# A layernorm's column factor and shift moved off the input: state weights, skip term and an outer product instead of two VectorE passes

## The chip, the cores and the metric

One core of one Trainium2 chip runs the whole program. The metric is the device time of one execution in microseconds, the median of three runs. All traces are of one profiled execution on that core.

## The reference

The program is one block of a network: a state-space convolution and an MLP mixer, each behind a layernorm that is modulated by a condition vector `c`. Only the first half matters here, with x of 2048 rows by 512 columns:

```python
sa, ca, ga = rows 0, 1, 2 of (silu(c) @ w_mod).reshape(6, 512)
h = layernorm(x) * (1 + ca) + sa
K[d, l] = Re sum_n C[d,n] * exp(dt[d] * A[d,n] * l) * dt[d] * B[d,n]     # 128 states n, 2048 taps l
y = irfft(rfft(pad(h)) * rfft(pad(K))) + h * Dskip                        # along the 2048 rows
x = x + ga * y
# second half: layernorm, a token mixer with w1 and w2, an MLP with w3 and w4
```

`1 + ca`, `sa` and `ga` hold one number for each of the 512 columns d. A factor on column d can stand at h, at K and Dskip, or at y: the convolution is linear in each.

## The kernel before, in words

The program runs in three stages, and each engine executes its instructions in the order in which the code is written (`manual_schedule`). Every engine waits only for what an instruction needs, and for the tile buffer that it writes to come free.

**Prologue (to about 40 us).** It loads and prepares the state parameters: decay rates in `TES`, phases in `T0S` and `T1S`, the magnitudes of the products C·dt·B as `wn`, and the first condition rows (`mods[0]` is sa, `mods[1]` is 1 + ca, `mods[2]` is ga, each spread over 128 partitions).

**The loop over 32 steps k (L554 to L587, about 40 to 213 us).** It makes the kernel K (16 columns of d a step) and, at its side, the first transform of u (16 blocks of 128 rows). In a step:

- `turns(k+2, 0)` and `turns(k+2, 1)`: TensorE forms phases in two PSUM tiles named xx (pool `psx`, two buffers; 8 matmuls for the sine half, 10 for the cosine half), and ScalarE takes their sine into a tile tr (three buffers).
- `products(k)`: VectorE multiplies tr with the magnitudes p into e0 and e1 (two buffers each): two passes on L476, one each on L485 and L486, and on even k one more on L482.
- `burst(k)`: TensorE contracts e0 with e1 in 32 small matmuls (64 in the trace) into a PSUM tile kp; after odd k ScalarE copies kp to KX.
- Every fourth step (k = 1, 5, ... 25, called `fresh`) also makes the next magnitudes: `exps` puts five groups of matmuls through the same two xx buffers, and ScalarE loads its exponential table, makes five tiles p, loads the sine table again, and goes on. The first two groups stand ahead of `burst(k)`, three behind it. `fill` matmuls (L492) stand between them and compute nothing that is used.
- `side[k]` holds work for step k: `u_stats` (mean and variance of a block of u on VectorE, the inverse root on GpSimd), `u_norm` (two VectorE passes, L425 and L426), `u_dft` (matmuls of two normalised blocks with the matrix FU into two PSUM tiles named pu, L435), and three times `mod_parts` and `mod_sum`, which make later condition rows through the same pool. That pool, `psu`, has two buffers; one `u_dft` takes both. The copies out of pu (`evict`, `later`) are ScalarE work written at the start of the next step, followed by SyncE DMAs to the DRAM tile VU.

**Stages two and three** (spectra and inverse transform to about 350 us, then mixer and MLP) are not touched by the change.

In step 1 the kernel before multiplies `mods[1]` and `mods[0]` by `mods[2]` (L584, L585), so that u already carries ga.

Of the kernel before, what the change touches and what calls it, by code (L numbers as in the profile page):

```python
# [27 lines left out]
def shape_constants():  # L28
# [10 lines left out]
    FU = FU.reshape(128, 2, 2, 2, 32).transpose(0, 1, 2, 4, 3)  # L39
    FK = np.zeros((2, 2, 32, 2, 64))  # L40
# [40 lines left out]
    for e in range(16):  # L81
# [8 lines left out]
        FU=FU.reshape(128, 256), FK=FK.reshape(128, 128), T2=T2, T3=T3, G=Gm,  # L90
# [21 lines left out]
def body(ctx, tc, A):  # L112
# [88 lines left out]
    WN = ph.tile([128, 512], F32, name="WN")  # L201
    modu = ph.tile([128, 3, 512], F32, name="modu")
# [82 lines left out]
    with tc.manual_schedule():  # L285
# [15 lines left out]
        Y.dma_start(FK, A["FK"])  # L301
        V.memset(cst, MAGIC)
# [105 lines left out]
        V.tensor_tensor(as4(wn), as4(wn), by(dt), op=OP.mult)  # L408
    pr.close()
# [9 lines left out]
    def u_stats(b):  # L419
        ul[b] = ln_stats(wk, [ut[b // 4][:, b % 4]], "lu")  # L420

    def u_norm(b):
        x = ut[b // 4][:, b % 4]
        mv, r = ul.pop(b)
        V.scalar_tensor_tensor(x, x, mv[:, 0, 0:1], mods[1], op0=OP.subtract, op1=OP.mult)  # L425
        V.scalar_tensor_tensor(x, x, r[:, 0:1], mods[0], op0=OP.mult, op1=OP.add)  # L426

    def u_dft(b, cp2):
        x = ut[b // 4]
        ps = [psu.tile([128, 512], F32, name="pu") for h in range(2)]  # L430
        for i in range(2):
            for h in range(2):
                q = 64 * (1 - i if h == 0 else i)
                j = slice(32 * JB[2 * h + cp2], 32 * JB[2 * h + cp2] + 32)
                T.matmul(ps[h][q:q + 64], FU[j, h, cp2 * 64:cp2 * 64 + 64], x[j, b % 4 + i],  # L435
                         start=True, stop=True, skip_group_check=True)

        def evict():
            vs = uv.tile([128, 2, 512], F32, name="vs")
            for h in range(2):  # L440
                act(vs[:, h], ps[h])
                c0 = h * 32 + cp2 * 16 + (14 - b if h == 0 else b)
                for i in range(2):
                    Y.dma_start(dram(VU, (c0 + i) * 256, [[16384, 64], [1048576, 2], [1, 256]]),
                                vs[i * 64:i * 64 + 64, h].rearrange("p (a d) -> p a d", a=2))
        later.append(evict)
# [22 lines left out]
    def products(k):  # L469
# [7 lines left out]
        if k == 0:  # L477
            weigh(0)
# [47 lines left out]
    at = lambda i: 1 + (i * 28) // 16  # L526
    for i in range(16):
        side[max(at(i) - 2, 0)].append(lambda i=i: u_stats(i))
        side[at(i)].append(lambda i=i: u_norm(i))
        if i % 2 == 1:  # L530
            side[at(i) + 1].append(lambda i=i: u_dft(i - 1, 0))
            side[at(i) + 2].append(lambda i=i: u_dft(i - 1, 1))
        if i % 4 == 3 and i < 8:
            side[at(i) + 2].append(lambda i=i: load_u(i // 4 + 2))
# [5 lines left out]
    with tc.manual_schedule():  # L540
# [5 lines left out]
        act(WN, wps)  # L546
# [7 lines left out]
        for k in range(33):  # L554
# [3 lines left out]
            if k + 2 < 32:  # L558
                turns(k + 2, 0)
                turns(k + 2, 1)  # L560
            if k < 32:
# [8 lines left out]
                burst(k, *e)  # L570
                if k == 31:
                    warm(4)
                if fresh:
                    KP[1] = psk.tile([128, 8, 64], F32, name="kp")
                    fill(3)
                    for u in range(2, 5):
                        exps(k // 4 + 1, u, u + 1)
                        if u < 4:
                            fill(1)
                    act(turn1, hpi, AF.Sin)  # L580
                if k % 4 == 3 and k < 28:
                    weigh(k // 4 + 1)
            if k == 1:
                V.tensor_mul(mods[1], mods[1], mods[2])  # L584
                V.tensor_mul(mods[0], mods[0], mods[2])  # L585
# [684 lines left out]
```

## Time and profile before

| | |
|---|---|
| median of three runs | 714.12 us (712.26 to 717.0) |
| the profiled execution | 714.44 us, span of its instructions 712.6 us |
| TensorE / VectorE / ScalarE busy over the span | 94% / 71% / 47% |
| VectorE busy between 60 and 200 us | 19.55 to 19.82 us of each 20 us |
| ScalarE busy between 60 and 200 us | 17.26 to 18.36 us of each 20 us |
| granted TensorE clock | 0.83 from 20 to 40 us, 1.00 from there to 300 us |

Busy shares are averages over a stretch; a busy TensorE includes modelled ends of pipelined matmuls, so it can look full while it waits. In rows of a timeline the first number is the start, the second the time, both in us. VectorE and ScalarE start an instruction about 0.1 us before the one ahead has ended, so what an instruction costs is the distance between starts.

### The profile page before, as it was taken

Reading aid. Unit: us, or ns where it says so; the run is one execution under the profiler, and the core shown is the slowest. Engines: PE = TensorE matmul, PEld = TensorE weight load, DVE = VectorE, ACT = ScalarE, POOL = GpSimd, SP = SyncE. Lnnn points to the kernel's source line nnn. Section 1 sums busy time; section 2 is a strip of 40 time slices with the busy share of each in tenths; the row PEclk is TensorE's granted clock in tenths of the full one; section 3 lists DMA queues with packets and bytes.
Section 4 is the critical chain, followed back from the end, with each engine's and each line's share of the span. In section 5 each row is a group of like instructions: output and inputs, shape, how many; then the busy total and the mean of one; then the engine's idle time right before and its main releaser. Section 6 shows DMA issues by size and latency. Waiting matters only on the chain.

```text
span 712.6 us, 16838 instructions
## 1 busy us (share of the span) xinstructions
PE 669.5 (94%) x7083; PEld 516.9 (73%) x7083; DVE 506.6 (71%) x847; ACT 335.5 (47%) x549; POOL 86.7 (12%) x191
## 2 busy tenths in 40 slices
PE   2689999999999999998999899999999999999997
PEld 1256555656569665664688889999898988989896
DVE  8889999999996666866988868557464636454422
ACT  3769888889866444533344623314123221212120
POOL 1011211112000000000473100101010000000000
PEclk9899999999999999999999999999999999999999
DMA  8451374653439999874659201011020101111011
GB/s 280 145 144 52 91 218 101 181 139 94 141 75 332 237 301 302 267 241 152 204 176 319 90 22 39 16 45 31 27 63 16 53 22 31 31 30 30 0 30 30
DMA packets 56627, 85.51 MB, mean 120 GB/s; under 512 B 5508, under 2 KB 43400, under 8 KB 54888
## 3 DMA queue, kind: packets, MB, share of 16 engines
q1 hardware_dynamic: 52536, 66.87, 33.2%
q0 software_dynamic: 3136, 16.52, 6.5%
q8 instruction: 56, 0.92, 0.6%
q10 hardware_dynamic: 880, 1.05, 0.5%
q14 instruction: 19, 0.16, 0.1%
HBM read 58.20 MB, written 31.85 MB: 126 GB/s over the span
## 4 chain that ended last, share of the span: by engine, by line
PE 47%; DMA 2%; DVE 2%; ACT 1%; issue 1%; SPq 1%; ACTq 0%; DVEq 0%
PE pm L824 7%; PE pm L825 7%; PE pm L827 7%; PE pa L948 6%; PE pa L940 6%; PE pa L941 6%; PE ph L878 2%; PE ph L879 2%; PE ph L881 2%; PE pT L789 2%; DMA ld<-ZT 1%; DMA GD<-go 1%; PE pT L1138 1%; PE py L721 1%; DMA win<-GD 0%
## 5 line engine op out<-in xcount | busy, mean ns | idle before, releaser
L120 ACT ACTIVATE gh<-pm 128x512 fp32r<-128x512 f32 (+1 forms) x48 | 26.9, 561 | 200.6 <-PE pm L827 200.6
L824 PE MATMUL pm<-nh,w3h 128*128 128x256 f32 (+1 forms) x352 | 85.8, 279 | 0.9 <-ACT nh L120 0.9
L825 PE MATMUL pm<-nh,w3l 128*128 128x256 f32 (+1 forms) x352 | 85.6, 279 | 0.1
L932 DVE TENSOR_TENSOR gl<-gf,gh 128x512 fp32r<-128x512 f32 (+1 forms) x48 | 30.9, 643 | 68.3 <-ACT gf L120 68.3
L940 PE MATMUL pa<-w4h,gh 128*128 128x512 f32 (+1 forms) x176 | 69.6, 395 | 0.0
L941 PE MATMUL pa<-w4l,gh 128*128 128x512 f32 (+1 forms) x176 | 68.9, 392 | 0.0
L824 PEld LDWEIGHTS pm<-nh,w3h 128*128 128x128 f32 (+1 forms) x352 | 65.3, 185 | 2.6 <-ACT nh L120 1.1
L825 PEld LDWEIGHTS pm<-nh,w3l 128*128 128x128 f32 (+1 forms) x352 | 65.2, 185 | 2.2 <-DVE w3l L743 0.5
L827 PE MATMUL pm<-nl,w3h 128*128 128x256 f32 (+1 forms) x352 | 54.8, 277 | 0.0
L948 PE MATMUL pa<-w4h,gl 128*128 128x512 f32 (+1 forms) x176 | 48.1, 390 | 0.8 <-DVE gl L932 0.8
L458 PE MATMUL xx<-MG,ON 64*128 64x512 f32 x160 | 47.0, 389 | 0.0
L459 PE MATMUL xx<-MG,ON 64*128 64x512 f32 x160 | 47.0, 389 | 0.0
L827 PEld LDWEIGHTS pm<-nl,w3h 128*128 128x128 f32 (+1 forms) x352 | 46.6, 185 | 0.2 <-DVE nl L797 0.2
L752 POOL TENSOR_TENSOR rs<-mv,eps_t 128x1 f32<-128x1 f32 (+1 forms) x39 | 11.9, 306 | 278.0 <-DVE mv L758 266.1
L884 DVE TENSOR_TENSOR h<-h,ph 128x512 f32<-128x512 f32 x16 | 11.0, 688 | 45.1 <-PE ph L881 45.1
L476 DVE SCALAR_TENSOR_TENSOR e<-tr,p 128x512 f32<-128x512 f32 x64 | 41.1, 683 | 1.8 <-ACT tr L120 1.8
L120 ACT ACTIVATE z<-pz 128x512 f32<-128x512 f32 x32 | 17.4, 594 | 51.4 <-issue 21.7
L677 DVE TENSOR_TENSOR ma<-pk,us 128x512 f32<-128x512 f32 x32 | 21.9, 686 | 26.8 <-issue 15.8
L508 PEld LDWEIGHTS kp<-e,e 128*32 128x32 f32 x2048 | 30.1, 110 | 12.9 <-issue 7.2
L948 PEld LDWEIGHTS pa<-w4h,gl 128*128 128x128 f32 (+1 forms) x176 | 33.0, 188 | 8.3 <-DVE gl L932 1.2
L485 DVE TENSOR_TENSOR e<-tr,p 128x1024 f32<-128x1024 f32 x32 | 39.0, 1218 | 0.0
L486 DVE TENSOR_TENSOR e<-tr,m 128x1024 f32<-128x1024 f32 x32 | 39.0, 1218 | 0.0
(234 smaller groups left out, 1755.6 us busy)
## 6 DMA issues: line engine op xcount, KB each, us to landing
VU<-vs SPq DMA_DIRECT2D x64, 128.0 KB, 3.2
ld<-VU SPq DMA_DIRECT2D x16, 512.0 KB, 14.1
ZT<-z POOLq DMA_DIRECT2D x15, 512.0 KB, 7.1
ld<-ZT SPq DMA_DIRECT2D x12, 512.0 KB, 5.5
Dw<-in_w POOLq DMA_DIRECT2D x8, 688.0 KB, 4.7
xu<-in_u SPq DMA_DIRECT2D x16, 256.0 KB, 5.7
KX<-in_u SPq DMA_DIRECT2D x16, 256.0 KB, 12.3
GD<-go SPq DMA_DIRECT2D x16, 256.0 KB, 2.5
```

The source lines that it names most:

```text
L120: return S.activation(out, in_, f, bias=bias, scale=scale)
L458: T.matmul(x[:, :512], la, ma, start=(i == 0), stop=(i == len(ops) - 1))
L459: T.matmul(x[:, 512:], lb, mb, start=(i == 0), stop=(i == len(ops) - 1))
L476: V.scalar_tensor_tensor(e0[:, 1, a], tr[:, 1, 0], 1.0 - 2.0 * a, mg[:, a], op0=OP.mult, op1=OP.mult)
L485: V.tensor_mul(e0[:, 0], tr[:, 0, 0:1].to_broadcast([128, 2, 512]), mg)
L486: V.tensor_mul(e1.rearrange("p r d q -> p r (d q)"), tr[:, :, 1], m1s[0][:, u % 2:u % 2 + 1].to_broadcast([128, 2, 512]))
L824: T.matmul(p, wh[:, k, c], hi[k], start=(k == 0), stop=False)
L825: T.matmul(p, wl[:, k, c], hi[k], start=False, stop=False)
L827: T.matmul(p, wh[:, k, c], lo[k], start=False, stop=(k == 3))
L940: T.matmul(acc[i], gh[:m, e, s], W4h[:m, f], start=(f == 0), stop=False)
L941: T.matmul(acc[i], gh[:m, e, s], W4l[:m, f], start=False, stop=False)
L948: T.matmul(acc[i], gl[:m, e, s], W4h[:m, f], start=False, stop=(f == 10))
```

## The change

- `u_norm` is one `tensor_scalar` (subtract the mean, multiply by the inverse root) instead of two passes with tensors.
- 1 + ca and ga go elsewhere: `mods[2]` becomes their product (three VectorE passes at the end of the prologue, with 1e-12 put where 1 + ca is zero), the state weights WN are multiplied by it where they leave PSUM (a VectorE pass in step 0 in place of a ScalarE copy), and the skip weights DS in step 1 (four passes of one partition).
- sa / (1 + ca) enters inside `u_dft`: a reciprocal and a product in step 1 (`shift_rows`), split into high and low parts in rows 0, 32 and 64 of `SHS` and `F1S` (two ScalarE copies at the start of step 2, two small VectorE subtractions, `shift_low`, at its end). Each `u_dft` starts with two matmuls F1S x SHS, and its four old ones accumulate onto them.
- The blocks of u are normalised and transformed at other steps. In six of the seven fresh steps the first `u_dft` of a pair (table `mid`) stands where `fill(3)` stood, between the second and third group of `exps`; the second of the pair follows at the next step.
- In steps k = 2, 6, 10, ... `turns(k+2)` stands behind `burst(k)` instead of ahead of it.

```diff
@@ shape_constants
+    F1 = np.zeros((96, 128))
+    F1[::32] = np.tile(W.sum(0).T.reshape(64), 2)
@@ tiles and loads
+    F1 = ph.tile([96, 128], F32, name="F1")
+    F1S = ph.tile([96, 128], F32R, name="F1S")
+    SHS = ph.tile([96, 512], F32R, name="SHS")
...
+        Y.dma_start(F1, A["F1"])
@@ end of the prologue
         V.tensor_tensor(as4(wn), as4(wn), by(dt), op=OP.mult)
+        V.tensor_scalar(ws, mods[1], 0.0, 1e-12, op0=OP.is_equal, op1=OP.mult)
+        V.tensor_add(mods[1], mods[1], ws)
+        V.tensor_mul(mods[2], mods[2], mods[1])
@@ def u_norm(b):
-        V.scalar_tensor_tensor(x, x, mv[:, 0, 0:1], mods[1], op0=OP.subtract, op1=OP.mult)
-        V.scalar_tensor_tensor(x, x, r[:, 0:1], mods[0], op0=OP.mult, op1=OP.add)
+        V.tensor_scalar(x, x, mv[:, 0, 0:1], r[:, 0:1], op0=OP.subtract, op1=OP.mult)
+
+    def shift_low():
+        V.tensor_sub(SHS[64:96], mods[0][64:96], SHS[64:96].bitcast(F32))
+        V.tensor_sub(F1S[32:64], F1[32:64], F1S[32:64].bitcast(F32))
+
+    def shift_rows():
+        V.reciprocal(mods[1], mods[1])
+        V.tensor_mul(mods[0], mods[0], mods[1])
+        later.append(lambda: act(SHS, mods[0][:96]))
+        later.append(lambda: act(F1S, F1))
@@ def u_dft(b, cp2):
         ps = [psu.tile([128, 512], F32, name="pu") for h in range(2)]
+        for h in range(2):
+            T.matmul(ps[h], F1S, SHS, start=True, stop=False, skip_group_check=True)
...
-                         start=True, stop=True, skip_group_check=True)
+                         start=False, stop=True, skip_group_check=True)
@@ def products(k):
         if k == 0:
+            by_d = lambda z: z.rearrange("p (b a c) -> p b a c", b=32, a=4)
+            V.tensor_mul(by_d(WN), by_d(wps), mods[2].rearrange("p (a b c) -> p b a c", a=4, b=32))
             weigh(0)
@@ side work
-    at = lambda i: 1 + (i * 28) // 16
-    for i in range(16):
-        side[max(at(i) - 2, 0)].append(lambda i=i: u_stats(i))
-        side[at(i)].append(lambda i=i: u_norm(i))
-        if i % 2 == 1:
-            side[at(i) + 1].append(lambda i=i: u_dft(i - 1, 0))
-            side[at(i) + 2].append(lambda i=i: u_dft(i - 1, 1))
...
+    for i, k in enumerate((1, 2, 3, 4, 7, 8, 10, 12, 14, 16, 18, 20, 22, 24, 26, 27)):
+        side[max(k - 2, 0)].append(lambda i=i: u_stats(i))
+        side[k].append(lambda i=i: u_norm(i))
+    mid = {}
+    for i, k in enumerate((3, 5, 9, 13, 17, 21, 25, 28)):
+        if k % 4 == 1:
+            mid[k] = lambda i=i: u_dft(2 * i, 0)
+        else:
+            side[k].append(lambda i=i: u_dft(2 * i, 0))
+        side[k + 1].append(lambda i=i: u_dft(2 * i, 1))
...
@@ the loop
-        act(WN, wps)
...
-            if k + 2 < 32:
+            early = k % 4 != 2
+            if k + 2 < 32 and early:
                 turns(k + 2, 0)
                 turns(k + 2, 1)
...
                 burst(k, *e)
+                if k + 2 < 32 and not early:
+                    turns(k + 2, 0)
+                    turns(k + 2, 1)
...
-                    fill(3)
+                    mid.get(k, lambda: fill(3))()
...
             if k == 1:
-                V.tensor_mul(mods[1], mods[1], mods[2])
-                V.tensor_mul(mods[0], mods[0], mods[2])
+                shift_rows()
+                for j in range(4):
+                    r = slice(32 * j, 32 * j + 1)
+                    V.tensor_mul(DS[r], DS[r], mods[2][r, j * 128:j * 128 + 128])
+            if k == 2:
+                shift_low()
```

How the order of instructions moves, at two places. First TensorE in step 13, a fresh step, and the start of step 14; before the change:

```order
L257 MATMUL xx<-CE,TES 128x512 x4
L508 MATMUL kp<-e_1556,e_1557 32x64 x32
L492 MATMUL kp<-CE,TES 128x512 x3
L257 MATMUL xx<-CE,TES 128x512 x2
...
L252 MATMUL xx<-CE,TES 128x256
L228 MATMUL pu<-wm,sp_91 128x512
L458 MATMUL xx<-C_105,T0S 128x512
```

and with it (L530 is the burst, L450 and L455 are `u_dft`, L233 is `mod_sum`):

```order
L262 MATMUL xx<-CE,TES 128x512 x4
L530 MATMUL kp<-e_1578,e_1579 32x64 x32
L450 MATMUL pu<-SHS,F1S 128x512 x2
L455 MATMUL pu<-xu,FU 64x512 x4
L262 MATMUL xx<-CE,TES 128x512 x2
...
L257 MATMUL xx<-CE,TES 128x256
L233 MATMUL pu<-wm,sp_91 128x512
L530 MATMUL kp<-e_1654,e_1655 32x64 x32
L478 MATMUL xx<-C_105,T0S 128x512
```

A `u_dft` now stands where three fills stood; `mod_sum`, which needs one of the two pu buffers, follows that `u_dft` with no ScalarE copy of it written in between, and the next burst stands between `mod_sum` and the next `turns`.

Second VectorE from the end of step 1 to `products(3)`, before the change:

```order
L584 TENSOR_TENSOR modu<-modu 128x512
L585 TENSOR_TENSOR modu<-modu 128x512
L425 SCALAR_TENSOR_TENSOR xu<-xu,lum,modu 128x512
L426 SCALAR_TENSOR_TENSOR xu<-xu,lur,modu 128x512
L476 SCALAR_TENSOR_TENSOR e_639<-tr,p_264 128x512 x2
L482 TENSOR_TENSOR m_643<-p_250 128x1024
L485 TENSOR_TENSOR e_639<-tr,p_264 128x1024
L486 TENSOR_TENSOR e_640<-tr,m_643 128x1024
```

and with it:

```order
L441 RECIPROCAL modu<-modu 128x512
L442 TENSOR_TENSOR modu<-modu 128x512
L615 TENSOR_TENSOR DS<-DS,modu 1x128 x4
L434 TENSOR_SCALAR xu<-xu,lum,lur 128x512
L149 BN_STATS lus<-xu 128x6
L150 BN_AGGR lum<-lus 128x2
L496 SCALAR_TENSOR_TENSOR e_635<-tr,p_268 128x512 x2
L504 TENSOR_TENSOR m_639<-p_254 128x1024
L507 TENSOR_TENSOR e_635<-tr,p_268 128x1024
L508 TENSOR_TENSOR e_636<-tr,m_639 128x1024
L437 TENSOR_TENSOR SHS<-modu,SHS 32x512
L438 TENSOR_TENSOR F1S<-F_113,F1S 32x128
```

The reciprocal, the skip weights and the statistics of a further block now stand ahead of `products(2)`, and `shift_low` ahead of `products(3)`.

More of the change, by code (lines that the diff above doesn't have):

```diff
@@ L89, in shape_constants @@
     return {k: f(v) for k, v in dict(
-        FU=FU.reshape(128, 256), FK=FK.reshape(128, 128), T2=T2, T3=T3, G=Gm,
+        FU=FU.reshape(128, 256), F1=F1, FK=FK.reshape(128, 128), T2=T2, T3=T3, G=Gm,
         FI=FI.reshape(128, 16 * 128), C0=C0, C1=C1, CE=CE, PA=PA.reshape(128, 512), PB=PB.reshape(128, 2048), ID=np.eye(128)).items()}
@@ L525, in body @@
         side[k + 1].append(lambda n=n: later.append(mod_sum(n)))
-    at = lambda i: 1 + (i * 28) // 16
-    for i in range(16):
-        side[max(at(i) - 2, 0)].append(lambda i=i: u_stats(i))
-        side[at(i)].append(lambda i=i: u_norm(i))
-        if i % 2 == 1:
-            side[at(i) + 1].append(lambda i=i: u_dft(i - 1, 0))
-            side[at(i) + 2].append(lambda i=i: u_dft(i - 1, 1))
-        if i % 4 == 3 and i < 8:
-            side[at(i) + 2].append(lambda i=i: load_u(i // 4 + 2))
+    for i, k in enumerate((1, 2, 3, 4, 7, 8, 10, 12, 14, 16, 18, 20, 22, 24, 26, 27)):
[8 more added lines that the diff above has]
+        side[k + 1].append(lambda i=i: u_dft(2 * i, 1))
+        if i in (1, 3):
+            side[k + 2].append(lambda i=i: load_u(i // 2 + 2))
     def add_skip(h, g0, g1):
```

## The prediction

> **What bounds the kernel now.** The change works in the loop over 32 steps, so I first read the busy times by stretch, 20 us each (columns: length, PE, PEld, DVE, ACT, POOL with their instructions, clock, DMA share, GB/s):
>
> ```profile
> 60.00:80.00 20.00, 19.25 (x356) 12.39 (x356) 19.82 (x27) 17.69 (x21) 3.43 (x5) 1.00 0.36 91
> ```
>
> VectorE is full. If it set the pace, work taken from it would come straight off the time. So the second view is the timeline of one round, from the burst of step 6 to that of step 10, on TensorE (most rows left out):
>
> ```profile
> 83.70 1.10 PE L508 MATMUL kp<-e,e 128*32 128x64 f32 x64
> 87.39 1.10 PE L508 MATMUL kp<-e,e 128*32 128x64 f32 x64
> 88.42 1.09 PE L435 MATMUL pu<-xu,FU 32*64 32x512 f32 x8
> 91.70 1.10 PE L508 MATMUL kp<-e,e 128*32 128x64 f32 x64
> ...
> 96.11 0.73 PE L257 MATMUL xx<-CE,TES 32*128 32x512 f32 x2
> 97.29 0.73 PE L257 MATMUL xx<-CE,TES 32*128 32x512 f32 x2 [0.45 <-ACT tr L120]
> 97.95 1.10 PE L508 MATMUL kp<-e,e 128*32 128x64 f32 x64
> ...
> 101.96 0.51 PE L252 MATMUL xx<-CE,TES 128*128 128x512 f32 x2
> 105.07 1.10 PE L508 MATMUL kp<-e,e 128*32 128x64 f32 x64
> 106.10 1.09 PE L435 MATMUL pu<-xu,FU 32*64 32x512 f32 x8
> 107.12 0.49 PE L458 MATMUL xx<-C,T0S 64*128 64x512 f32 x1
> ```
>
> A burst takes 1.03 (105.07 to 106.10), a `u_dft` 1.02 (to 107.12), a pair of `turns` 91.70 - 88.42 - 1.02 = 2.26. From 88.42 to 97.95 these follow each other with no room: burst, `u_dft`, `turns`, burst, `u_dft`, `turns`, two groups of magnitudes; the one wait is 0.45 for ScalarE. The rest of the round waits for ScalarE too:
>
> ```profile
> 98.55 4.91 ACT L120 ACTIVATE p<-xx 128x1024 f32<-128x1024 f32 x5
> 103.48 1.28 ACT L120 ACT_TABLE_LOAD   x1
> 104.88 0.58 ACT L120 ACTIVATE KX<-kp 128x512 f32<-128x512 f32 x1
> 105.36 1.02 ACT L120 ACTIVATE tr<-xx 128x1024 f32<-128x1024 f32 x1
> 107.29 1.09 ACT L120 ACTIVATE vs<-pu 128x512 f32<-128x512 f32 x2
> ```
>
> Five exponentials through two xx buffers fix when each group of magnitudes may start; a sine read takes 0.9 to 1.1. With these durations alone, and no VectorE in it, the round from the burst at 83.70 to that at 105.07 comes out as 21.4 us, which is what it took. VectorE's rows beside it:
>
> ```profile
> 40.53 1.29 DVE L476 SCALAR_TENSOR_TENSOR e<-tr,p 128x512 f32<-128x512 f32 x2 [1.84 <-ACT tr L120]
> ...
> 75.06 1.29 DVE L476 SCALAR_TENSOR_TENSOR e<-tr,p 128x512 f32<-128x512 f32 x2
> ...
> 79.67 0.74 DVE L425 SCALAR_TENSOR_TENSOR xu<-xu,lum,modu 128x512 f32<-128x512 f32 x1
> ...
> 81.20 0.69 DVE L147 BATCH_NORM_STATS2 lus<-xu 128x6 f32<-128x512 f32 x1
> ...
> 84.36 1.21 DVE L486 TENSOR_TENSOR e<-tr,m 128x1024 f32<-128x1024 f32 x1
> ```
> The burst of step 7 did not wait for VectorE: its products ended at 84.36 + 1.21 = 85.6, the burst came at 87.39. TensorE and ScalarE, tied by the two xx buffers, set the pace; VectorE is full at nearly the same pace, but 1 to 3 us ahead.
>
> **The change part by part.** VectorE first, where two groups are wanted, the pass of another layernorm and the prologue's reciprocal, and for short passes a third:
>
> ```profile
> L906 DVE TENSOR_SCALAR h<-h,mv,rs 128x512 f32<-128x512 f32 x14 | 7.0, 542 | 0.0
> L372 DVE RECIPROCAL tp_mx<-tp_mx 128x512 f32<-128x512 f32 x1 | 3.4, 3353 | 0.0
> L309 DVE MEMSET cst<- 1x128 f32 x6 | 1.0, 165 | 0.4
> ```
>
> An even step's products take 79.67 - 75.06 = 4.61 (an odd step's 3.47, without L482), a `u_norm` 81.20 - 79.67 = 1.53, statistics 0.82. The new pass has the form of L906: 7.0 us / 14 = 0.5. That frees 16 x 1.03 = 16.5 us. Added: the reciprocal 3.3, DS 0.6 (four passes of 1 x 128, by the last row), WN 0.25 later than the copy was, `shift_low` 0.8; one product less, 0.6. Net VectorE gives back 12 us, two per round; but by the reading above the round does not wait for it, so I price this at nothing, but for some tenths. The three passes at the prologue's end lie under the idle 1.84 ahead of 40.53, where VectorE waits for the first sine; uncovered they would cost that much.
>
> *Start of the loop (steps 1 to 5).* Here VectorE gets the new work before it gets the savings.
>
> ```profile
> 51.13 0.68 DVE L584 TENSOR_TENSOR modu<-modu 128x512 f32<-128x512 f32 x1
> ```
> ```profile
> 55.16 1.10 PE L508 MATMUL kp<-e,e 128*32 128x64 f32 x64
> ...
> 59.16 0.51 PE L252 MATMUL xx<-CE,TES 128*128 128x512 f32 x2
> 62.27 1.10 PE L508 MATMUL kp<-e,e 128*32 128x64 f32 x64
> 65.98 1.10 PE L508 MATMUL kp<-e,e 128*32 128x64 f32 x64
> ...
> 76.55 1.10 PE L508 MATMUL kp<-e,e 128*32 128x64 f32 x64
> ```
> ```profile
> 62.09 0.58 ACT L120 ACTIVATE KX<-kp 128x512 f32<-128x512 f32 x1
> ```
>
> From 51.4: reciprocal 3.3, product 0.6, DS 0.6, `u_norm` 0.5, statistics 0.8, `products(2)` 4.6: ready at 61.9. Burst 2 now stands ahead of `turns(4)`; TensorE is free for it at 59.6 and waits 2.3 us, with `turns(4)` behind it. `shift_low` waits for the ScalarE copy of SHS, behind KX at 62.09 (63.2), so `products(3)` ends at 68.8: burst 3 at 68.85 instead of 65.98. The `u_dft` behind it takes 1.5 (below), burst 4 waits for `products(4)` until 74.25, then `u_dft`, `turns(7)`, two groups: burst 5 at about 81.0 against 76.55, **+4.4**.
>
> *The two new matmuls.* 32 in all; no row has this shape, the nearest is L458, whose pairs follow each other by 0.23. Below: that, 0.46 for two. Above: 0.5 each, if they run as the plain ones of L228 do (1.02 for two, next fence). I take 0.48, nearer in type to L458: a `u_dft` becomes 1.5.
>
> *A steady round, by hand.* From the start of the last group of magnitudes (0): burst 0.44 to 1.47; `turns` to 3.73. The second `u_dft` needs the pu buffers of the first. Their copies stand on ScalarE behind the last exponential (to 1.5), the table (2.8) and KX (to 3.4); the first ends at 4.0, so TensorE starts at 4.1 and ends at 5.8. Then `turns` 8.1, burst 9.1, `turns` 11.4, burst 12.4, `turns` 14.7, two groups, the second after the cosine read at 15.9, burst 16.6 to 17.6, the moved `u_dft` to 19.1 (three fills took 0.9 there), and the last group at 21.3. **21.3 against 21.4**: the 0.9 of fills and a wait of 0.4 go, two longer `u_dft`s and a new wait of 0.4 come.
>
> *`mod_sum` and `mod_parts` in psu.* In step 13 `mod_sum` stands behind the `u_dft` of that step and needs its buffer, so TensorE waits from 0.44 to 4.1 with the burst and `turns(16)` behind it, and ScalarE idles in turn for its next phases.
>
> ```profile
> 120.23 1.10 PE L508 MATMUL kp<-e,e 128*32 128x64 f32 x64
> 124.58 1.02 PE L228 MATMUL pu<-wm,sp 128*128 128x512 f32 x2
> 141.69 1.10 PE L508 MATMUL kp<-e,e 128*32 128x64 f32 x64
> 164.18 1.10 PE L508 MATMUL kp<-e,e 128*32 128x64 f32 x64
> 186.28 1.10 PE L508 MATMUL kp<-e,e 128*32 128x64 f32 x64
> 206.85 1.10 PE L508 MATMUL kp<-e,e 128*32 128x64 f32 x64
> 212.02 1.10 PE L508 MATMUL kp<-e,e 128*32 128x64 f32 x64
> ```
>
> Then 1.0 for itself, burst, `turns` to 8.4, `u_dft` to 9.9, where the plain round stood at 5.8: 21.3 + 4.1 = 25.4 for steps 13 to 17, against 141.69 - 120.23 = 21.46, **+3.9**. In step 26 `mod_parts` comes between the two `u_dft`s: it starts at 4.1 and takes 1.0, and the second half of the `u_dft` waits for its copy until 7.0. With a `u_dft` more than before in this round (steps 25, 26, 28), burst 29 comes 24.3 after burst 25, against 20.57: **+3.7**.
>
> The other rounds: steps 5 to 9 -0.1; 9 to 13 the same within 0.1; 17 to 21 21.3 + 2.0 for `mod_parts` and `mod_sum` = 23.3 against 22.49, +0.8 (before they lay partly in waits); 21 to 25, one `u_dft` less, 21.3 against 22.10, -0.8. Tail, burst 29 to 31: 1.03 + 1.5 + 1.03 + 2.1 of warming matmuls = 5.7 against 5.17, +0.5.
>
> Sum: 4.4 - 0.1 + 0 + 3.9 + 0.8 - 0.8 + 3.7 + 0.5 = **+12.4**. On the profiled 714.44 that is 726.8; the median of the runs lies 0.3 lower: **726.5**. What comes after the loop only shifts. F1's load and the moved DMAs are hidden: the DMA share is 0.36 in the stretch above.
>
> **Rivals.** (1) *VectorE is the bound after all*, place: the 40 to 212 us in which it hardly idles; price: the 12 us net. Time 702. It decides if bursts wait for products; against it stand the slack of 1.8 at burst 7 and the round that closes without VectorE. The Trainium skill, Perfetto Trace Analysis, Identifying the Most-Contended Engine, says to take the engine with the highest occupancy as the one to relieve first; by it the result is this rival's, and the row at 60 us (19.82 of 20) agrees with the occupancy but the burst rows do not with the pace.
> (2) *The moved `u_dft` shortens the round*: if the waits of 0.4 at 3.7 and of 0.5 before the second group fall away, and the third group of magnitudes starts no later than before, up to 1.3 a round over seven is 9 us, against the 12.4: about 717, no change. For it: 0.9 of fills was pure waiting. Against: the exponentials on ScalarE then wait 0.7 for TensorE.
> (3) *The psu waits hide*, if the copies come earlier than I place them: 3.7 in step 13 and 1.4 in step 26 go, 721.4.
> (4) *The clock drops in the wait of step 13*, TensorE being idle 3.7 us. In the prologue a wait of 3.85 was followed by matmuls at half pace:
>
> ```profile
> 30.66 3.50 PE L228 MATMUL pu<-xu,sp 128*128 128x512 f32 x4 [3.85 <-ACT xu L120]
> ```
>
> 3.50 for four here, 1.02 for two at 124.58. One such stretch costs 1.5 to 3.5 us more: about 729. The Trainium skill, TensorE: Matmul & The Clock Gate, Part 1, gives an idle window of about 3.4 us that runs freely; by it a wait of 3.7 seldom holds a whole one.
>
> **How the numbers follow.** Forecast (720 to 728) 0.54, rival 4 0.12, rival 3 0.08 (half of it over 1%), rival 2 0.16, rival 1 0.10. A measurement of this kernel can tell about 1%, 7 us. Faster by over 1%: 0.10; slower: 0.54 + 0.12 + 0.04 + 0.03 (rival 2 in part) = 0.73; within 1%: 0.17. The range goes from 711, which leaves rival 1 out, to 735, where the new matmuls take 0.5 each (32 x 0.27 = 9 us more).
>
> **What would show it.** Right: VectorE no longer full between 90 and 200 us, yet rounds of 21 us; burst 2 waiting for products about 2 us; a gap of 3 to 4 us on TensorE before `mod_sum` in step 13, ended by ScalarE's vs; an idle stretch in ScalarE there; the loop ending near 225. Wrong: rounds near 19.5 us (rival 1), or rounds of 20 to 20.5 (rival 2).

## The result: 735.35 us, 2.9% slower, and the profile after

The changed kernel takes 735.35 us (median of four runs, 733.81 to 737.47) beside 714.83 for the kernel before in runs on the same chip: a ratio of 1.0291, 95% interval 1.0245 to 1.0336. The forecast was 726.5 with a range of 711 to 735: the direction and most of the places were right, but the change costs 20.5 us and not 12.4, and the time lies just above the range.

All of it lies in the loop. The start of the burst of step k can be read in the timeline of TensorE, and the distances between the bursts of fresh steps are the rounds of the prediction (us; the last column tells where the granted clock was 0.50 in the changed kernel):

| round | before | predicted | after | half clock in it, from (length) |
|---|---|---|---|---|
| burst 1 to 5 | 21.39 | 25.8 | 27.67 | 60.9 (6.8) |
| 5 to 9 | 21.40 | 21.3 | 21.61 | |
| 9 to 13 | 22.28 | 22.3 | 23.35 | 108.7 (3.4) |
| 13 to 17 | 21.46 | 25.4 | 28.60 | 132.6 (10.2) |
| 17 to 21 | 22.49 | 23.3 | 23.48 | |
| 21 to 25 | 22.10 | 21.3 | 21.60 | |
| 25 to 29 | 20.57 | 24.3 | 26.29 | 214.5 (3.4) |
| 29 to 31 | 5.17 | 5.7 | 5.78 | |
| sum | 156.9 | 169.4 | 178.4 | |

The profiled execution took 736.13 us (span 734.3, mean clock 0.974) against 714.44. Burst 1 starts at 55.06 (before 55.16), and behind burst 31 there remain 734.3 - 233.44 = 500.9 us (before 712.6 - 212.02 = 500.6). So the 21.5 us by which the loop grew are nearly the whole difference of 21.7. The rounds here and below are of one profiled execution of each kernel. The four executions of the changed kernel had mean clocks of 0.974 (the profiled one) to 0.984, so the places of the half clock may differ from one execution to the next.

The same view by stretch, with the columns of before, and three stretches that matter:

```profile
60.00:80.00 20.00, 17.18 (x278) 11.82 (x280) 19.29 (x28) 12.43 (x18) 2.74 (x5) 0.83 0.24 64
120.00:140.00 20.00, 16.13 (x246) 8.89 (x246) 14.19 (x20) 14.57 (x18) 3.94 (x6) 0.81 0.37 106
180.00:200.00 20.00, 19.78 (x358) 12.63 (x346) 15.66 (x22) 17.08 (x22) 3.40 (x5) 1.00 0.49 142
```

VectorE, 19.8 of 20 us before, now has 4.3 us free in the third row, where nothing is disturbed; the round there (21 to 25, with one `u_dft` less than before) still takes 21.60. In the first two rows the clock column reads 0.83 and 0.81, where before it read 1.00: a second loss beside the waits. TensorE's timeline from burst 5 to 6, the counterpart of the rows shown of before:

```profile
82.73 1.10 PE L530 MATMUL kp<-e,e 128*32 128x64 f32 x64
83.77 0.73 PE L450 MATMUL pu<-SHS,F1S 96*128 96x512 f32 x2
84.43 1.09 PE L455 MATMUL pu<-xu,FU 32*64 32x512 f32 x8
85.45 0.73 PE L262 MATMUL xx<-CE,TES 32*128 32x512 f32 x2
```

Here the moved `u_dft` follows the burst where three fills stood. Its start-to-start parts are 0.66 for the two outer products and 1.02 for the old matmuls: 1.68, where I had 1.5.

The waits came where they were predicted. TensorE, steps 2 and 13 and the second half of the `u_dft` of step 26:

```profile
62.54 1.93 PE L530 MATMUL kp<-e,e 128*32 128x64 f32 x64 [2.98 <-DVE e L508]
136.64 2.07 PE L233 MATMUL pu<-wm,sp 128*128 128x512 f32 x2 [3.39 <-ACT vs L122]
213.09 0.49 PE L450 MATMUL pu<-SHS,F1S 96*128 96x512 f32 x1 [1.39 <-ACT wm L122]
```

And VectorE's rows that make burst 2 late:

```profile
51.28 3.35 DVE L441 RECIPROCAL modu<-modu 128x512 f32<-128x512 f32 x1
55.34 1.16 DVE L615 TENSOR_TENSOR DS<-DS,modu 1x128 f32<-1x128 f32 x4
56.52 0.55 DVE L434 TENSOR_SCALAR xu<-xu,lum,lur 128x512 f32<-128x512 f32 x1
63.09 0.68 DVE L437 TENSOR_TENSOR SHS<-modu,SHS 32x512 fp32r<-32x512 f32 x1 [0.61 <-ACT SHS L122]
```

What the predicted sum did not have is in the first two of the wait rows: a burst takes 1.93 instead of 1.10, `mod_sum` 2.07 instead of 1.02. The same timeline some steps later, without any wait in it (the `turns` behind it left out):

```profile
105.37 0.73 PE L450 MATMUL pu<-SHS,F1S 96*128 96x512 f32 x2
106.03 1.09 PE L455 MATMUL pu<-xu,FU 32*64 32x512 f32 x8
107.05 0.73 PE L262 MATMUL xx<-CE,TES 32*128 32x512 f32 x2
107.71 0.49 PE L514 MATMUL kp<-CE,TES 128*128 128x512 f32 x1
108.13 0.79 PE L262 MATMUL xx<-CE,TES 32*128 32x512 f32 x2
108.85 0.79 PE L514 MATMUL kp<-CE,TES 128*128 128x512 f32 x1
109.44 0.84 PE L257 MATMUL xx<-CE,TES 128*128 128x512 f32 x2
110.21 1.94 PE L530 MATMUL kp<-e,e 128*32 128x64 f32 x64
```

From 108.7 on a fill takes 0.79 for 0.49 and the burst 1.94 for 1.10, though TensorE had not paused. By stretch, the 3.4 us ahead of each of the four half-clock stretches, and two of these themselves (clock is the third column from the end):

```profile
57.50:60.90 3.40, 2.06 (x7) 0.97 (x6) 3.37 (x6) 3.19 (x5) 1.44 (x2) 1.00 0.00 0
105.30:108.70 3.40, 3.40 (x27) 1.27 (x15) 3.10 (x6) 2.47 (x3) 0.26 (x2) 0.99 0.77 311
108.70:112.10 3.40, 3.40 (x70) 2.55 (x69) 3.40 (x5) 2.92 (x4) 0.95 (x1) 0.50 0.01 4
129.20:132.60 3.40, 3.40 (x17) 1.39 (x16) 3.37 (x6) 2.41 (x4) 1.98 (x3) 0.99 0.02 5
132.60:142.80 10.20, 6.81 (x79) 4.17 (x79) 1.66 (x3) 5.16 (x9) 0.00 (x0) 0.50 0.44 121
211.10:214.50 3.40, 2.01 (x14) 0.58 (x10) 2.92 (x4) 1.93 (x3) 0.00 (x0) 1.00 0.73 154
```

The four are of two kinds. Ahead of 108.7 and 132.6, in fresh steps, TensorE was busy for all of 3.40 us, for most of the time with matmuls on 32 rows. The stretch at 132.6 begins before the wait of 3.39 ahead of `mod_sum` (133.25 to 136.64): that wait did not start it. Ahead of 60.9 and 214.5 TensorE was busy for 2.06 and 2.01 us only: the stretch at 60.9 begins inside the wait of burst 2 (59.56 to 62.54), behind step 1, whose fills the change keeps, and the one at 214.5 behind the wait of 1.39 in step 26. The matmuls that the change took out of the fresh steps are the fills:

```profile
L492 PE MATMUL kp<-CE,TES 128*128 128x512 f32 x35 | 13.7, 457 | 0.0
```
```profile
L514 PE MATMUL kp<-CE,TES 128*128 128x512 f32 x17 | 8.2, 504 | 0.0
```

(groups by line, 43 to 215 us, of before and of the changed kernel): 18 of 35 are gone, three in each of six fresh steps. So the theory for the experiments: the predicted chain of waits, plus a clock that falls because fills that compute nothing kept it up. The rivals: VectorE is the bound after all; the clock falls because of the waits alone; the loss is the change's arithmetic or its places alone.

### The profile page after: what moved, and what is told of

Read it like the earlier page. It is cut to its first block, busy times and chain, and to the rows that moved or that the text cites. A ratio compares the mean times of both kernels' runs of the same rounds, so it can differ in the third digit from the quotient of the medians.

```text
span 734.3 us, 16832 instructions
## 1 busy us (share of the span) xinstructions
PE 686.0 (93%) x7097; PEld 527.3 (72%) x7097; DVE 499.4 (68%) x841; ACT 336.3 (46%) x550; POOL 86.2 (12%) x191
## 4 chain that ended last, share of the span: by engine, by line
PE 46%; DMA 2%; DVE 2%; ACT 1%; issue 1%; SPq 0%; ACTq 0%; DVEq 0%
PE pm L856 7%; PE pm L857 7%; PE pm L859 7%; PE pa L980 5%; PE pa L972 5%; PE pa L973 5%; PE ph L910 2%; PE ph L911 2%; PE ph L913 2%; PE pT L821 2%; DMA GD<-go 1%; PE py L753 1%; PE pT L1170 1%; DMA ld<-ZT 1%; PE pm L753 0%
## 5 line engine op out<-in xcount | busy, mean ns | idle before, releaser
L478 PE MATMUL xx<-MG,ON 64*128 64x512 f32 x160 | 49.4, 406 | 0.0
L479 PE MATMUL xx<-MG,ON 64*128 64x512 f32 x160 | 49.3, 406 | 0.0
L530 PEld LDWEIGHTS kp<-e,e 128*32 128x32 f32 x2048 | 32.3, 116 | 15.7 <-issue 8.5
L122 ACT ACTIVATE tr<-xx 128x1024 f32<-128x1024 f32 x32 | 32.9, 1030 | 18.8 <-PE xx L479 16.9
L122 ACT ACTIVATE p<-xx 128x1024 f32<-128x1024 f32 (+1 forms) x40 | 37.8, 980 | 6.8 <-PE xx L262 5.6
L530 PE MATMUL kp<-e,e 128*32 128x64 f32 x2048 | 37.7, 229 | 3.0 <-DVE e L508 3.0
```

What stands on the lines that cost most here:

```text
L122: return S.activation(out, in_, f, bias=bias, scale=scale)
L478: T.matmul(x[:, :512], la, ma, start=(i == 0), stop=(i == len(ops) - 1))
L479: T.matmul(x[:, 512:], lb, mb, start=(i == 0), stop=(i == len(ops) - 1))
L530: T.matmul(kp[32 * j:32 * j + 32, (k % 2) * 4 + g], e1[:, r, d], e0[:, r, :, d * 32:d * 32 + 32], start=(r == 0), stop=(r == 1), skip_grou ...
```

## The experiments

Times are medians; ratios are against the kernel before on the same chip. Rounds are given in the table's order.

**Is VectorE the bound?** The kernel before, with one normalising pass and nothing else of the change; it leaves the factor 1 + ca, ga and the shift out of u:

```diff
-        V.scalar_tensor_tensor(x, x, mv[:, 0, 0:1], mods[1], op0=OP.subtract, op1=OP.mult)
-        V.scalar_tensor_tensor(x, x, r[:, 0:1], mods[0], op0=OP.mult, op1=OP.add)
+        V.tensor_scalar(x, x, mv[:, 0, 0:1], r[:, 0:1], op0=OP.subtract, op1=OP.mult)
```

> The kernel before with the one-pass u_norm alone: the factor 1 + ca, ga and the shift are left out of u, nothing else moves. VectorE has 16 us less to do in the loop. Chain theory (TensorE and ScalarE set the rounds): rounds stay at 21.3 to 22.3 us, the time falls by 1 to 3 us, to 712 to 714; VectorE shows idle time of some 15 us in the loop. Rival (VectorE is the bound): rounds of about 19.3 us, 698 to 700.

713.03 us, ratio 0.9984 (0.996 to 1.0008); rounds 21.40, 21.41, 21.85, 21.43, 22.50, 21.61, 20.57, 5.16. VectorE by stretch:

```profile
60.00:80.00 20.00, 19.18 (x353) 11.92 (x349) 18.83 (x25) 17.63 (x21) 3.41 (x5) 1.00 0.37 91
160.00:180.00 20.00, 19.52 (x359) 11.85 (x355) 17.87 (x23) 18.20 (x22) 3.08 (x6) 1.00 0.50 146
```

The sixteen normalisations take 8.6 us of VectorE instead of 23.9 (busy time of their lines, 43 to 215 us), and the rounds agree with those of before within 0.5 us; from burst 1 to 31 they are 0.9 us shorter together. VectorE was full because it kept pace, not because it set it.

**Is it the waits that drop the clock?** The changed kernel with fills put into the two longest waits:

```diff
+                if k == 2:
+                    fill(10)        # ahead of burst(2)
...
+            if k == 13:
+                fill(12)            # ahead of mod_sum
```

> The changed kernel with 10 fill matmuls ahead of the burst of step 2 and 12 ahead of mod_sum in step 13, where TensorE waits anyway; they compute nothing that is used. Clock theory (a wait of TensorE is followed by stretches of half clock, which cost some 5 us after these two waits): the half-clock stretches near 61 to 68 and 132 to 143 us go, burst 1 to burst 5 falls from 27.7 to about 25.8 us, burst 13 to burst 17 from 28.6 to about 25.4, the time from 735 to about 730. Rival (the time is in the waits themselves and in the longer u_dft alone): the waits stay, the rounds stay at 27.7 and 28.6, the time stays at 735 or rises by what the fills stick out.

734.24, ratio 1.028 (1.023 to 1.033), against about 730 expected: hardly a gain in the time. The rounds are 26.22, 21.61, 22.46, 25.72, 25.46, 25.30, 27.90, 5.78; the two that were aimed at come out about as expected. TensorE still comes to `mod_sum` and to burst 2 when it did (timeline):

```profile
136.27 1.12 PE L233 MATMUL pu<-wm,sp 128*128 128x512 f32 x2 [0.78 <-ACT vs L122]
137.32 1.10 PE L530 MATMUL kp<-e,e 128*32 128x64 f32 x64
```

but `mod_sum` takes 1.12 and the burst 1.10: the stretches at 60.9 and 132.6 are gone, and rounds 1 to 5 and 13 to 17 are 1.45 and 2.9 shorter. In their place stand stretches of half clock at 158.3, 199.2 and 216.3 (3.4, 3.4 and 6.8 us), and these rounds are 2.0, 3.7 and 1.6 longer. This was the slowest of the kernel's four executions (739.58, the others 732.89 to 734.54), so these losses need not stand in all of them. Only the stretch at 158.3 lies behind the burst of a fresh step, one whose three fills are gone; the longest pause ahead of it is 0.45. Ahead of the one at 199.2 TensorE stands still for 1.96 us, for nothing that the profile shows, and the one at 216.3 stands where 214.5 stood. So the wait of burst 2 did cost the clock, and fills in it keep the clock up; in step 13 the fills stand behind the matmuls that ran ahead of 132.6, and whether they or a shift in time removed that stretch is not shown. The clock can also fall without such a wait (158.3): the rival explains a part of it.

**The psu waits.** The other conditions' matmuls in steps where no moved `u_dft` shares the pool:

```diff
-        k = 7 * n - 9
+        k = 8 * n - 17
```

> The changed kernel with the three pairs of mod_parts and mod_sum at steps 7 and 8, 15 and 16, 23 and 24 instead of 12 and 13, 19 and 20, 26 and 27, so that none stands between two u_dfts and their copies. Psu theory: the round of steps 13 to 17 falls from 28.6 to about 23.6, that of 25 to 29 from 26.3 to about 21, the other rounds trade 1 to 2 us among themselves; the time falls by about 10 us to 725. Rival (the loss is the two new matmuls in each u_dft, 16 times 0.7 us, and the collision costs little): under 3 us, 732 or more.

731.27, ratio 1.0238 (1.0193 to 1.0282). Rounds 27.76, 23.48, 21.61, 24.49, 21.60, 23.48, 21.34, 5.77: 8.9 us less in the loop. The waits of steps 13 and 26 are gone (25 to 29 falls from 26.29 to 21.34), and with the second the stretch at 214.5. But half clock stays at 61.3, where burst 2 still waits, and comes at 132.9, for 3.4 us. At 132.9 TensorE has no wait, the moved `u_dft` stands in the window ahead as at 108.7, and the round still takes 24.49. Behind burst 31 remain 503.6 us, 2.7 more than in the changed kernel, with a stretch of half clock at 262.6: a part of why the time fell by less than the loop and missed the 725 expected.

**Fills kept everywhere.** That kernel, with the three fills kept behind the moved `u_dft` and ten ahead of burst 2:

```diff
+                if k == 2:
+                    fill(10)
...
-                    mid.get(k, lambda: fill(3))()
+                    mid.get(k, lambda: None)()
+                    fill(3)
```

> The kernel of e2 (mod_parts and mod_sum moved) with three fills again in each fresh step, behind the u_dft that took their place, and ten fills ahead of the burst of step 2. Clock theory (a fresh step without fills, 32-row matmuls and waits only, lets the granted clock halve by chance of where its windows fall): no half-clock stretch is left between 40 and 230 us, the start up to burst 5 falls by about 1.5 us against e2, each later fresh round is 0.9 longer by the fills; time 730 to 733. Rival (the half clock has another cause): half-clock stretches stay, and the time rises by the fills to 735 to 737.

733.16, ratio 1.0256 (1.0214 to 1.0298), just above the 730 to 733 expected. Rounds 26.25, 24.41, 22.48, 24.42, 22.48, 24.38, 22.23, 5.78. From burst 1 to burst 31 the clock is 1.00 throughout: with the fills, none of the stretches is left. But a round now holds fills and `u_dft` one after the other, 0.87 more than 21.61, so the loop gains only 6.0 us on the changed kernel.

**What are the fills worth by themselves?** The kernel before, without any of them:

```diff
-                    fill(3)
...
-                        if u < 4:
-                            fill(1)
```

> The kernel before without its fill matmuls (five in each of seven fresh steps); nothing that is used is left out. By the waits alone the rounds are unchanged, since the magnitudes wait for ScalarE. Clock theory: without the fills the granted clock halves at some fresh steps, 3.4 us or more each time, and the time rises by 2 to 8 us, to 717 to 723. Rival (fills are only waiting): 714 to 715 and clock 1.00 in the loop.

730.88, ratio 1.0237 (1.0201 to 1.0274), beside 715.58: 15 us slower for taking out work that computes nothing, 11.8 of them in the loop of the profiled execution. That is more than I expected. Rounds 23.12, 21.85, 24.50, 23.64, 24.70, 22.82, 22.91, 5.14, and half clock in each of the seven fresh steps (59.4, 83.3, 103.8, 127.7, 151.6, 178.9, 199.4; 3.4 or 6.8 us). Before and without fills, the loop by stretch:

```profile
40.00:220.00 180.00, 172.32 (x3001) 109.50 (x2999) 172.67 (x226) 150.87 (x183) 26.66 (x40) 1.00 0.47 126
```
```profile
40.00:220.00 180.00, 168.42 (x2666) 103.33 (x2665) 164.27 (x213) 147.10 (x173) 26.96 (x40) 0.89 0.42 111
```

And TensorE's timeline in one such step, where the longest wait is 0.58 (it is busy for 2.43 of the 3.40 us ahead of 83.3):

```profile
79.54 1.10 PE L508 MATMUL kp<-e,e 128*32 128x64 f32 x64
81.23 0.73 PE L257 MATMUL xx<-CE,TES 32*128 32x512 f32 x2 [0.58 <-ACT p L120]
82.14 0.73 PE L257 MATMUL xx<-CE,TES 32*128 32x512 f32 x2 [0.18 <-ACT p L120]
83.07 0.80 PE L252 MATMUL xx<-CE,TES 128*128 128x512 f32 x2 [0.21 <-ACT p L120]
```

No VectorE work, no pool and no outer product is changed here, and the clock falls. The Trainium skill, TensorE: Matmul & The Clock Gate, Part 1, has the clock go to 4/8 after an idle window of about 3.4 us that runs freely. The levels and lengths agree (0.50, and stretches of 3.4, 6.8 and 10.2 us); that the window must be idle does not, neither here nor at 108.7 of the changed kernel. The measurement decides: windows in which TensorE executes for 2.4 to 3.4 of 3.4 us, mostly matmuls on a part of the array's rows or columns, were enough.

Over all fourteen traces, between the burst of a fresh step and its last group of magnitudes: in the seven kernels that keep every fill no stretch of half clock begins there, in 49 such steps; in the six kernels that lack three fills in six steps it does in 7 of 36 (in two of these, of the kernel with the new places and the old arithmetic below, 0.4 and 1.4 us behind the burst, so that most of the window ahead lies before it); in the kernel without any in 6 of 7, and in the seventh 0.5 us later. So the fills hold the clock there, and without them it can fall but need not.

**The start.** The changed kernel without the reciprocal, to see what makes burst 2 late:

```diff
-        V.reciprocal(mods[1], mods[1])
```

> The changed kernel without the reciprocal in step 1 (the shift row is sa times 1 + ca instead of sa over 1 + ca). Theory (VectorE is late at the start of the loop, and the wait of burst 2 costs the clock too): burst 2 comes about 3 us earlier, the half-clock stretch from 61 to 68 us shrinks or goes, burst 1 to burst 5 falls from 27.7 to 23 to 24.5 us, the time to 730 to 732. Rival (the start is slow for the reordered turns alone): burst 1 to burst 5 stays above 26, the time at 734 or more.

733.8, ratio 1.0279 (1.022 to 1.0339). Rounds 26.24, 21.62, 22.44, 28.62, 23.48, 21.60, 26.34, 5.78. The first was expected at 23 to 24.5. Burst 2 comes at 58.35 and waits no more, and no half clock follows, which again ties the stretch at 60.9 to that wait. Yet the round gains nothing but the clock's 1.4, since burst 3 now waits (TensorE, then VectorE):

```profile
67.81 1.10 PE L529 MATMUL kp<-e,e 128*32 128x64 f32 x64 [2.30 <-DVE e L507]
```
```profile
61.95 0.68 DVE L437 TENSOR_TENSOR SHS<-modu,SHS 32x512 fp32r<-32x512 f32 x1 [4.10 <-ACT SHS L122]
```

`shift_low` waits 4.10 us for the ScalarE copy of SHS, with `products(3)` behind it. So, next, the same with `shift_low` moved behind `products(3)`:

```diff
-            if k == 2:
+            if k == 3:
                 shift_low()
```

> The kernel of e4 (no reciprocal) with shift_low behind products(3) instead of ahead of it, so that VectorE does not wait there for the copy of SHS. Theory (reciprocal and shift_low hide each other): burst 3 no longer waits for products, burst 1 to burst 5 falls from 26.2 in e4 to 23.5 to 24.5 us, the time to 730 to 732. Rival (the start is long for the longer u_dfts and the order of turns): burst 1 to burst 5 stays above 25.5.

732.68, ratio 1.0244 (1.0203 to 1.0285). The first round falls from 26.24 to 23.40, about as expected; the time is just above the 730 to 732. The reciprocal, which by the wait of 2.98 looked worth 3 us, is worth nothing but the clock while `shift_low` stands where it does; what moving `shift_low` alone is worth was not run. In this execution the half clock in round 13 to 17 begins at 130.8, inside the wait ahead of `mod_sum` (3.52): here a wait did start it.

**Arithmetic and places apart.** The change's arithmetic with the table of before, its fills and its order of `turns`:

```diff
+    at = lambda i: 1 + (i * 28) // 16        # side work placed as before
...
+            early = True
...
-                    mid.get(k, lambda: fill(3))()
+                    fill(3)
```

> The change's arithmetic alone: one-pass u_norm, factors in WN and DS, reciprocal and outer product, but u_norm, u_dft, fills and turns at the places of the kernel before. Theory: no half-clock stretch in the loop (fills kept, no collision in psu); each u_dft 0.66 longer, so rounds with two of them 22.5 to 22.8; the start up to burst 5 about 25, since products(3) stand behind shift_low, which waits for the copy of SHS; time 726 to 729. Rival (the arithmetic is cheap, the new places cost it all): 716 to 719.

730.3, ratio 1.0212 (1.017 to 1.0253); rounds 27.34, 22.76, 23.17, 22.78, 23.63, 26.16, 21.71, 5.78. The loop takes 173.3, 16.4 more than before; sixteen `u_dft`s that are 0.66 longer make 10.6 of it. The time was expected at 726 to 729 and the loop without half clock, and neither came. The start is no better than with the new places, against what I expected of it (25): burst 3 waits 2.32 for its products and half clock begins at 70.2, though every fill stands. A second stretch, at 196.5, stands in round 21 to 25, where a ScalarE copy waits for a DMA that still reads its tile (timeline), and the next sine comes 1.86 behind it:

```profile
195.23 1.09 ACT L122 ACTIVATE vs<-pu 128x512 f32<-128x512 f32 x2 [1.65 <-DMA VU<-vs]
```

And the change's places with the arithmetic of before (two passes, no outer product):

```diff
-        for h in range(2):
-            T.matmul(ps[h], F1S, SHS, start=True, stop=False, skip_group_check=True)
...                                    # u_norm, WN, DS and mods as before
```

> The change's places alone: u_norm, u_dft, mod and turns where the changed kernel has them, fills gone from six fresh steps, but the two-pass u_norm with its factors and shift, and no outer product. Theory: start up to burst 5 about 21.5 to 22.5; the round of 13 to 17 about 25 by the collision in psu and more with half clock; the others 21 to 21.6, now set by VectorE; half-clock stretches at some fresh steps; time 721 to 726. Rival (the new places are harmless or a gain): 712 to 716.

726.33, ratio 1.016 (1.0115 to 1.0206), about as expected; rounds 22.79, 20.74, 25.09, 26.53, 22.42, 20.49, 25.28, 5.13. Where nothing disturbs it a round is 0.7 shorter than before (20.74, and 20.49 in 21 to 25, which has one `u_dft` less): the moved `u_dft` does fill the fills' time, as rival 2 said. But half clock comes at 97.9 (10.2), 128.6 (6.8) and 193.4 (6.8), and the waits for the pool's buffers remain. So the places cost 11.6 in the loop, the arithmetic 16.4, and both together 21.5, not 28. That they share stretches and waits is my reading of it; no run separates these.

**Looking for a version that gains.** The column factor moved as in the change, but the shift added to u by another engine, the fills kept, and pairs of `u_dft` and the conditions' matmuls put where no two share the pool. First with GpSimd, which also takes the shift's product and the skip weights:

```diff
         V.tensor_scalar(x, x, mv[:, 0, 0:1], r[:, 0:1], op0=OP.subtract, op1=OP.mult)
+        P.tensor_tensor(x, x, mods[0], op=OP.add)
...
+    for i, (k, l) in enumerate(((3, 4), (6, 8), (10, 12), (14, 16), (18, 20), (22, 24), (26, 27), (28, 29))):
+        side[k].append(lambda i=i: u_dft(2 * i, 0))
+        side[l].append(lambda i=i: u_dft(2 * i, 1))
...
+            early = k % 4 != 2 or k == 2
```

> A third kernel: factors in WN and DS as in the change, but the shift is added to the normalised block by GpSimd, so there is no outer product; fills stay; the first u_dft of a pair stands in the wait of TensorE behind turns(k+2) at k = 6, 10, ..., 26, where turns now follow the burst, and the second two steps later; mod_parts and mod_sum moved clear of them; turns(4) ahead of burst 2 as before; DS products and the product with the reciprocal on GpSimd. Chain theory: a round loses the 0.8 us of two waits, some 20.6; time 707 to 711. Rival (VectorE or GpSimd becomes the bound, by GpSimd passes that hold u back or slow VectorE): rounds of 21.4 or more, time 714 or more.

719.75, ratio 1.0056 (1.003 to 1.0083), where a gain to 707 to 711 was expected; rounds 24.85, 21.10, 21.79, 22.33, 21.46, 21.46, 20.52, 6.01, no half clock. Groups by line, 43 to 215 us (count, busy and mean ns of one, idle before), of this kernel:

```profile
L493 DVE SCALAR_TENSOR_TENSOR e<-tr,p 128x512 f32<-128x512 f32 x62 | 47.5, 806 | 0.7 <-ACT tr L122 0.7
L435 POOL TENSOR_TENSOR xu<-xu,modu 128x512 f32<-128x512 f32 x16 | 44.2, 2765 | 29.2 <-DVE xu L434 26.0 <-PE pu L226 3.1
L434 DVE TENSOR_SCALAR xu<-xu,lum,lur 128x512 f32<-128x512 f32 x16 | 15.4, 963 | 0.0
```

and of the changed kernel:

```profile
L496 DVE SCALAR_TENSOR_TENSOR e<-tr,p 128x512 f32<-128x512 f32 x56 | 35.8, 682 | 24.0 <-ACT tr L122 23.7 <-issue 0.3
L434 DVE TENSOR_SCALAR xu<-xu,lum,lur 128x512 f32<-128x512 f32 x16 | 8.7, 541 | 0.0
```

A product pass grows from 682 to 806 ns and a normalising pass from 541 to 963 beside the GpSimd adds: 62 x 0.124 + 16 x 0.42 = 14 us come back to VectorE, somewhat more than the second pass took (12.0 in the kernel before). The Trainium skill, SBUF — State Buffer, SBUF: two separate sides, says that VectorE and GpSimd block each other at a shared pair of ports, when VectorE reads two inputs or runs in a two-port mode. The product pass reads two inputs and agrees with it; in which mode the normalising pass runs, no trace here shows. Then the same with the add as a second VectorE pass, and the factor still moved:

```diff
-        P.tensor_tensor(x, x, mods[0], op=OP.add)
+        V.tensor_tensor(x, x, mods[0], op=OP.add)
```

> The kernel of e8 with the shift added by a second VectorE pass instead of GpSimd, and the product with the reciprocal on VectorE too: two-pass normalisation of 1.1 us a block against 1.5 before. Chain theory (rounds are set by TensorE and ScalarE once VectorE has some slack, and the waits behind turns(k+2) take a u_dft): rounds of 20.5 to 20.9, start up to burst 5 of 22.5 to 24, time 709 to 713. Rival (VectorE still sets the round, or the start costs what the rounds save): 714 to 717.

714.43, ratio 0.9998 (0.9978 to 1.0018); rounds 23.93, 20.65, 21.48, 22.32, 21.46, 21.46, 20.53, 5.64. Without the GpSimd adds the two passes are back at 682 and 541 ns. Expected was a gain, and there is none: the start costs 2.5 more, the other rounds and the tail together 1.9 less. And the same places with the arithmetic of the kernel before:

```diff
         V.scalar_tensor_tensor(x, x, mv[:, 0, 0:1], mods[1], op0=OP.subtract, op1=OP.mult)
         V.scalar_tensor_tensor(x, x, r[:, 0:1], mods[0], op0=OP.mult, op1=OP.add)
...
+    for i, (k, l) in enumerate(((3, 4), (6, 8), (10, 12), (14, 16), (18, 20), (22, 24), (26, 27), (28, 29))):
...
+            early = k % 4 != 2 or k == 2
```

> The kernel before with its own arithmetic, u_norm, u_dft, mod and turns at the places of e8, fills kept. VectorE has 16.5 + 2 x 2.35 = 21.2 us of work in a round. Theory: rounds of 21.0 to 21.3 by VectorE, no half clock in the loop, time 711 to 714. Rival (places alone gain what TensorE's waits were): rounds of 20.6, 708 to 710.

714.75, ratio 1.0002 (0.9973 to 1.0032); rounds 21.39, 21.05, 21.90, 22.32, 21.46, 21.46, 20.54, 7.22. The rounds gain 1.6 and the tail gives 2.05 back, since VectorE, with two passes again, is late there (burst 30 waits 1.63 for its products). None of the variants beats the kernel before by more than its measurement can tell.

## Why the prediction was right in direction and short in size

- *VectorE's saving is worth nothing*: right, and shown (one normalising pass alone: 0.9984, and 0.9 us in the loop). The Trainium skill's rule on the engine with the highest occupancy (Perfetto Trace Analysis, Identifying the Most-Contended Engine) would have given 702; the burst rows, which did not wait for VectorE, were the better guide.
- *Start, +4.4*: the mechanism is right. Burst 2 waited 2.98 (2.3 predicted), the skip weights took 1.16, not 0.6, `shift_low` waited. 26.2 where the clock did not fall (with fills, or without the reciprocal), 25.8 predicted.
- *Steps 13 and 26*: right. `mod_sum` waited 3.39 for ScalarE's copy (3.7 predicted), the `u_dft` of step 26 1.39 (1.4). With the clock kept up, round 13 to 17 was 25.72 (25.4).
- *The `u_dft`, mis-sized*: 1.5 predicted, 1.68 measured. The two outer products take 0.66, where I took 0.48, from the range 0.46 to 1.0. One to three of them stand in a round: 5 to 9 took 21.61 (21.3), 21 to 25 21.60 (21.3). By round, what is left of each beside a run without half clock in it (in the first, the skip weights' 0.6 is part of it): 0.4 + 0.3 + 0.15 + 0.3 + 0.2 + 0.3 + 0.1, and for 25 to 29, where there is none, 3 x 0.18 = 0.5, is 2.3 us.
- *The other rivals.* The psu waits did not hide (3.39 and 1.39, rows above). The shorter round of rival 2 exists, 20.74 with the old arithmetic in the new places; with the outer products in it, the round is 21.61.
- *The clock, the step that failed.* The sum takes the clock as full in every round. Half clock stood only in rival 4, for the wait of step 13, at 1.5 to 3.5 us and a chance of 0.12, and rival 2 called the fills' 0.9 "pure waiting". Measured, the clock was at half in four places. At 108.7 and 132.6 it fell in fresh steps whose fills the change had taken away: 23.35 - 22.45 = 0.9 us and 28.60 - 25.72 = 2.9. The place and price of the second are those of rival 4, which is luck in part: the stretch began ahead of the wait. It was 10.2 us long, beside 3.4 where no `mod_sum` waits behind it (132.9, with the conditions moved). At 60.9 and 214.5 it fell at waits, of burst 2 and of the `u_dft` of step 26: rival 4's mechanism, in places for which it had no price. The first cost 27.67 - 26.22 = 1.4. For 214.5 there is no run with the same work and a full clock: 26.29 less the 24.3 predicted and the 0.5 above leaves about 1.5, which is an estimate. Together 6.7, of which some 3.8 go with the fills and some 2.9 with waits.

2.3 + 6.7 = 9.0 us is the distance between the predicted sum of rounds, 169.4, and the 178.4 measured.

What stays open is the rule by which the clock falls in some of these fresh steps and not in others: it stayed up at 84 us with the same matmuls in the same order, and the stretches moved to other steps when the work ahead shifted by one to three microseconds (the kernel with fills in the waits). The traces show two parts of an answer. In one execution the starts of the stretches lie whole multiples of 3.413 us apart (60.9, 108.7, 132.6 and 214.5 are 47.8, 23.9 and 81.9 us apart, 14, 7 and 24 of them), so it depends on how such windows fall on the program. And the windows ahead are light: counted as rows x columns x elements of their matmuls, those ahead of the 25 stretches that begin between burst 1 and burst 31 of the fourteen traces hold 29% to 56% of what the median of the other windows there holds. But 48 of the 613 others at full clock are as light and kept it, so this is not the whole rule, and no run here tests it.

## What to carry to other kernels

Matmuls that compute nothing can carry time: before an edit takes their place, ask what the granted clock would be without them, whether the work that replaces them, here transforms on 32 rows, is as dense, and whether the edit makes TensorE wait somewhere new. An engine at 99% in the profile can still be a follower; look whether anyone waits for its results before taking work from it. Where two late things wait in a row, taking one away shows nothing: the start of this loop fell by 1.4 us without the reciprocal, all of it clock, and by 2.8 more once the place of `shift_low` was changed as well.

## What the runs showed of the hardware that was not expected

The clock fell to 0.50 behind windows of 3.4 us in which TensorE was executing all the time (105.3 to 108.7). That is rare, 4 of the 25 stretches between burst 1 and burst 31 in the fourteen traces; in the windows ahead of the others TensorE was busy for 31% to 87%. It fell in all seven fresh steps of the kernel without fills: rounds to 24.7 us, 11.8 us more in the loop, though it has 35 matmuls less. Behind the loop, which no kernel changed, 499.1 to 501.7 us remain in seven of the profiled executions and 503.5 to 505.5 in the others; all but one of these have a half-clock stretch that starts between 252 and 273 us, and none of the seven has. So a total carries some 4 us that belong to no edit, and the rounds of the loop are the better measure here. A GpSimd add of 128 x 512 took 2765 ns and slowed VectorE's passes beside it by 18% and 78%.
